# Attention and two feed-forward layers on one core: batch 0's loads in buffers of their own, issued at the start on two queues

## Chip, cores and metric

The kernel runs on one core of one Trainium2 chip. The metric is device time in microseconds (us). Three runs of the kernel before gave a median of 914.42 us (913.56 to 915.66).

## What is computed

Three stages follow each other: an attention with two kinds of causal window, and two feed-forward layers that feed each other. Cut to what matters:

```python
# q, k, v: (4, 8, 576, 64); heads 0-3: window of 32; heads 4-7: every 4th key of the last 128
scores = scale * q @ k.T
scores = where(mask, scores, -1e9)
attn = exp(scores - max(scores)); attn /= sum(attn) + 1e-9
x = (attn @ v), heads joined                   # (2304, 512)
h = x @ w_in;  g = max(h, 0) + alpha * min(h, 0);  x = g @ w_out      # d_ff 2048
h = x @ w2_in; g = 0 for h <= -1, h for h >= 1, (h + 1)**2 / 4 between;  y = g @ w2_out
```

The weights arrive as float64 words and are made into float32 on the chip.

## The kernel before

**Attention.** A batch has six groups (`NGB`); a group is 3 super-blocks of 128 query rows with 64 keys each. Per group: `a_scores` (TensorE: 4 mask matmuls, 12 score matmuls; VectorE: the row maximum), `a_exp` (L133), `a_turn` (three transposes on TensorE, a copy on ScalarE), `a_values` (12 matmuls, then three VectorE operations), `a_out` (three transposes, copies into `X` on ScalarE). A group needs two operand tiles. `qk` holds queries and keys; its lower 64 partitions and its upper 64 partitions are loaded by one DMA each (`a_load_qk`, L96), the rest of the tile is zeroed by memsets at the start (L352, L353). `vz` holds the values and is loaded likewise (`a_load_v`, L102; memsets L354, L355). In batch 0 three buffers of each serve six groups, so a later group's load waits for the reads of an earlier one. All of these DMAs are issued by SyncE's queue, in program order.

**Weights.** A piece is a 128x512 block of float64 words, 512 KB. `w_load` (L193) brings it into `st` (two buffers), `w_make` (L199) gives three VectorE operations (L224, L225, L219), and `conv(k)` (L372) runs the next `k` of them; when a piece is done the next one's load is issued. A layer has 32 pieces, 96 operations. An input piece is then cut into a high and a low part (`w_cut`, L229, POOL making the low part), an output piece in `wo_split`.

**Feed-forward.** A layer has five token tiles; a tile has 16 slots (`NF`), one per 128 columns of d_ff. A slot runs `f_h` (12 matmuls), `f_g` (VectorE, and `gh` on ScalarE, L293), `f_cut`, and two slots later `f_y` (12 matmuls).

**Order.** The program is laid out by hand (`manual_schedule`): each engine runs its instructions in the order of the code. The start is the loop over the six groups of batch 0 (from L389), then the first matmuls of slots 0 and 1, with `conv` calls between. In the first tile, `conv` runs 1 operation in slot 0 (`EARLY[0]`), 6 in slot 1 and 6 in each later slot until the 32 pieces are made. Attention of the other batches is spread over the slots.

**Waits of DMAs.** Transfers issued on the hardware queues share eight completion semaphores, in turn. A DMA that takes a semaphore waits, on the engine that issues it, until the DMA that had the semaphore before has landed. These waits stand in the built program, not in the source.

Of the kernel before, what the change touches and what calls it, by code (L numbers as in the profile page):

```python
# [10 lines left out]
F32 = mybir.dt.float32  # L11
# [21 lines left out]
KW = 192  # L33
# [3 lines left out]
KQ = GS * KW  # L37
QK = KQ + GS * P
# [9 lines left out]
# operations that make weights: in the first two slots; inside f_g and before f_cut, by phase  # L48
EARLY = (1, 6)
BEFORE = ((0, 3), (1, 3))  # L50
# points from the scores of a group to its transposes, its values and its output
# [3 lines left out]
def _subs(sb):  # L55
    """The four (head pair, sub-block) of a super-block of a batch."""
    base = 0 if sb < NSB // 2 else 2
    n = 4 * (sb % (NSB // 2))
    return [(base + (n + j) // NSUB, (n + j) % NSUB) for j in range(4)]


def _key_offset(sb, j):
    return 32 * j + (32 if sb % (NSB // 2) == NSB // 4 and j >= 2 else 0)
# [3 lines left out]
def attention_then_two_ffns(ctx: ExitStack, tc: tile.TileContext, aqk, av, w1i, w1o, w2i, w2o, alpha, masks, ident, out):  # L67
# [22 lines left out]
    sc_t, s_t, pT_t, o_t = {}, {}, {}, {}  # L90

    def buf(i):
        """The first batch has three buffers for its operands, the others two."""
        return i % 3 if i < NGB else i % 2

    def a_load_qk(i):  # L96
        if i < NG:
            t = qk[buf(i)]
            nc.sync.dma_start(t[:D, :QK], aqk[i, :D])
            nc.sync.dma_start(t[D:, KQ:], aqk[i, D:])  # L100

    def a_load_v(i):  # L102
        if i < NG:
            for h in range(2):
                r = slice(h * D, (h + 1) * D)
                nc.sync.dma_start(vz[buf(i)][r, :, h].rearrange("p n j d -> p n (j d)"), av[i, r])

    def a_scores(i, pool, tag, add_on_pe):
        ps = pool.tile([P, GS, 2, KEYS], F32, tag=tag, name="s_ps")
        sb0 = (i % NGB) * GS  # L110
        t = qk[buf(i)]
        mk = mask[:, sb0:sb0 + GS, None, :].to_broadcast([P, GS, 2, KEYS])
        if add_on_pe:
            for j in range(4):
                r = slice(j * SUB, (j + 1) * SUB)
                nc.tensor.matmul(ps[r], idb[:, r], mk, start=True, stop=False)
        for n in range(GS):
            for j in range(4):
                k0 = _key_offset(sb0 + n, j)
                r = slice(j * SUB, (j + 1) * SUB)  # L120
                q = t[:, KQ + n * P + j * SUB:KQ + n * P + (j + 1) * SUB]
                k = bass.AP(t.tensor, t.offset + n * KW + k0, [t.ap[0], [QK, 2], [1, KEYS]])
                nc.tensor.matmul(ps[r, n], q, k, start=not add_on_pe, stop=not add_on_pe or n == GS - 1)
        s = tmp(i).tile([P, 2 * GS, KEYS], F32, tag="s", name="s")
        src = ps.rearrange("p n h k -> p (n h) k")
        if not add_on_pe:
            nc.vector.tensor_tensor(s.rearrange("p (n h) k -> p n h k", h=2), ps, mk, ALU.add)
            src = s
        mx = st_p.tile([P, 2 * GS], F32, tag="mx", name="mx")
        nc.vector.tensor_reduce(mx, src, AX.X, ALU.max)  # L130
        sc_t[i] = (src, s, mx)

    def a_exp(i):  # L133
        src, s, mx = sc_t.pop(i)
        nc.vector.tensor_scalar(mx, mx, -SCALE, None, ALU.mult)
        for n in range(2 * GS):
            nc.scalar.activation(s[:, n], src[:, n], AF.Exp, bias=mx[:, n:n + 1], scale=SCALE)
        s_t[i] = s
# [52 lines left out]
    wt, wo, cv, cut = {}, {}, {}, []  # L191

    def w_load(ph, f, part):  # L193
        w = ((w1i, w1o), (w2i, w2o))[ph][part]
        st = cv_p.tile([P, DM, 2], I32, tag="st", name="st")
        nc.sync.dma_start(st.rearrange("p a b -> p (a b)"), w[f].bitcast(I32))
        cv[ph, f, part] = st

    def w_make(ph, f, part):  # L199
        """The three operations that make a piece: sign and highest exponent bit, the 27 bits behind the  # L200
        three exponent bits that float32 lacks, the top of the low word (0 and float32's normal range)."""
        st = cv.pop((ph, f, part))
        top, low = st[:, :, 1], st[:, :, 0]
        if part:
            wf = wp.tile([P, DM], F32, tag=f"o{f}", name="wo")
            wo[ph, f] = wf
        else:
            hi = wp.tile([P, DM], F32R, tag=f"ih{f}", name="wih")
            lo = wp.tile([P, DM], F32R, tag=f"il{f}", name="wil")
            if (ph, f) == (0, 1):  # L210
                # the second piece is made before the first is cut
                wf = wp.tile([P, DM], F32, tag=f"o{NF - 1}", name="wf")
            else:
                wf = cv_p.tile([P, DM], F32, tag="wf", name="wf", bufs=1)
            wt[ph, f] = (hi, lo)
        wi = wf.bitcast(I32)

        def last():
            nc.vector.scalar_tensor_tensor(wi, low, 29, wi, ALU.logical_shift_right, ALU.bitwise_or)  # L219
            if not part:  # L220
                cut.append((wf, hi, lo))

        return [
            lambda: nc.vector.tensor_scalar(wi, top, 0x07FFFFFF, 3, ALU.bitwise_and, ALU.logical_shift_left),  # L224
            lambda: nc.vector.scalar_tensor_tensor(wi, top, -0x40000000, wi, ALU.bitwise_and, ALU.bitwise_or),  # L225
            last,
        ]
# [98 lines left out]
    def pieces(ph):  # L326
        """The order in which the weights are needed."""
# [5 lines left out]
    with tc.manual_schedule(), ExitStack() as late:  # L333
        first = ExitStack()
        sp = first.enter_context(tc.tile_pool(name="sp", bufs=1))
        qk.append(sp.tile([P, QK + KQ], F32, tag="qk2", name="qk2"))
        vz.append(sp.tile([P, GS, 2, 4, DS], F32, tag="vz2", name="vz2"))
# [11 lines left out]
        nc.scalar.activation(half, half, AF.Exp, scale=0.0)  # L349
        nc.scalar.activation(half, half, AF.Copy, scale=0.5)  # L350
        for i in range(3):
            nc.vector.memset(qk[i][:D, QK:], 0.0)  # L352
            nc.vector.memset(qk[i][D:, :KQ], 0.0)  # L353
            nc.gpsimd.memset(vz[i][:D, :, 1], 0.0)  # L354
            nc.gpsimd.memset(vz[i][D:, :, 0], 0.0)  # L355
        a_load_qk(0)
        a_load_qk(1)
        a_load_v(0)
        a_load_qk(2)
        a_load_v(1)  # L360
        a_load_v(2)
# [3 lines left out]
        # the tensor engine reaches its full clock while the first loads are under way  # L365
# [6 lines left out]
        def conv(k):  # L372
            """The next k operations that make weights; behind each piece another load starts."""
# [13 lines left out]
        # the attention of batch 0 alone; the first products run while its last heads are still under way  # L387
        n0 = order[0]
        for i in range(NGB):  # L389
            a_scores(i, ps_h, "h", True)  # L390
            a_load_qk(i + 3 if i < 5 else i + 2)
            if i < 2:
                w_load(*pend_l.pop(0))
            if i >= 3:
                a_out(i - 3, ps_y, f"y{2 + i % 2}")
            if i >= 1:
                a_turn(i - 1, ps_a, "a")
            a_exp(i)
            if i == 5:
                conv(1)  # L400
                w_cut(True)
                x_split(n0, 0, True)
                conv(1)
            if i >= 2:
                a_values(i - 2, ps_y, f"y{i % 2}")
                a_load_v(i + 1)
            if i == 3:
                conv(2)
        conv(1)
        a_values(4, ps_y, "y0")  # L410
        a_load_v(7)
        a_turn(5, ps_a, "a")
        a_out(3, ps_y, "y3")
        conv(1)
        x_split(n0, 1, True)
        w_cut(True)
        a_values(5, ps_y, "y1")
        a_out(4, ps_y, "y2")
        x_split(n0, 2)
        f_h(n0, 0, (0,))  # L420
        a_out(5, ps_y, "y3")
        x_split(n0, 3)
        f_h(n0, 0, (1,))
        f_h(n0, 1, (0, 1))
# [36 lines left out]
        for k in range(len(slots) + 2):  # L461
            n, f = slots[k] if k < len(slots) else (None, None)
            nn = order[k // NF + 1] if k // NF + 1 < len(order) else None
            # the results of a tile leave before the next but one needs its banks
# [11 lines left out]
            if n:  # L476
# [5 lines left out]
                elif n == n0:  # L482
                    ops = 6
# [46 lines left out]
def _attention_layout(q, k, v):  # L530
    """Super-blocks of four sub-blocks of 32 queries of a head pair; heads 4-7 by residue of the position."""
# [9 lines left out]
    ak = np.zeros((B, NSB, P, KW), q.dtype)  # L541
    av = np.ones((B, NSB, P, 4, DS), q.dtype)
    for sb in range(NSB):
        for j, (hp, s) in enumerate(_subs(sb)):
            p0 = s * SUB
            aq[:, sb, :, j * SUB:(j + 1) * SUB] = q[:, hp, :, p0:p0 + SUB].transpose(0, 1, 3, 2).reshape(B, P, SUB)
            k0 = _key_offset(sb, j)
            ak[:, sb, :, k0:k0 + KEYS] = k[:, hp, :, p0:p0 + KEYS].transpose(0, 1, 3, 2).reshape(B, P, KEYS)
# [5 lines left out]
    aq, ak, av = groups(aq), groups(ak), groups(av)  # L554
# [38 lines left out]
```

## Time and profile before

| | us |
|---|---|
| median of the runs | 914.42 |
| lowest and highest run | 913.56, 915.66 |
| span of the profiled execution | 912.2 |
| TensorE busy in it | 872.4 |
| VectorE busy | 543.0 |
| ScalarE busy | 338.3 |
| GpSimd busy | 264.3 |

The page gives the profiled execution by its span alone; the span is 2.2 us below the median of the runs, which also hold what lies around it. The engine shares are averages over the start (attention of batch 0), the first tile (weights are made), and the long rest.

### The profile page before, as it was taken

To read this page: it belongs to the slowest core of one execution; us is meant where nothing else is said; L and a number is where in the kernel's file an instruction comes from. 1 tells how busy PE (TensorE), PEld (TensorE's weight loads), DVE (VectorE), ACT (ScalarE), POOL (GpSimd) and SP (SyncE) were. 2 spreads that over 40 slices of the span, in tenths; PEclk is the share of its full clock that TensorE was granted. 3 is DMA by queue.
4 is the path that set the end of the run, shared out by engine and by line. 5 is a ranking of instruction groups with operands and counts; after the bars stand their busy time and mean duration, and the time that the engine had idled before them with its cause. 6 is when DMAs were issued, how large, how long until landed. Compare 5 with 4: busy or idle time off the path is not lost.

```text
span 912.2 us, 13342 instructions
## 1 busy us (share of the span) xinstructions
PE 872.4 (96%) x5194; PEld 716.2 (79%) x5194; DVE 543.0 (60%) x872; ACT 338.3 (37%) x693; POOL 264.3 (29%) x208
## 2 busy tenths in 40 slices
PE   6789888999999999999999999999999999999998
PEld 3567666788888888998777777888888888888898
DVE  3599999744455444447999897443354335433443
ACT  3533334433343332333222433343343334333454
POOL 3223333121221212443434343222212222222243
PEclk7999999999999999999999999999999999999999
DMA  9956654312213200000333131010001000100000
GB/s 224 229 178 198 188 178 155 78 41 50 70 40 79 65 1 1 1 1 27 135 126 129 69 139 70 1 47 0 1 1 47 0 1 1 47 1 0 29 19 24
DMA packets 26319, 61.38 MB, mean 67 GB/s; under 512 B 2976, under 2 KB 12736, under 8 KB 26256
## 3 DMA queue, kind: packets, MB, share of 16 engines
q1 hardware_dynamic: 26080, 60.16, 22.6%
q8 instruction: 41, 0.67, 0.3%
q0 software_dynamic: 176, 0.37, 0.2%
q14 instruction: 22, 0.18, 0.1%
HBM read 55.80 MB, written 4.72 MB: 66 GB/s over the span
## 4 chain that ended last, share of the span: by engine, by line
PE 72%; DVE 18%; DMA 5%; issue 3%; ACT 1%; SPq 1%; POOL 0%; ACTq 0%; DVEq 0%
PE h_ps L274 12%; PE y L311 11%; PE h_ps L276 11%; PE h_ps L275 11%; PE y L312 11%; PE y L313 11%; DVE wo L225 4%; DVE gl L299 2%; DMA st<-w1i 2%; DVE wo L219 2%; DMA vz<-av 2%; DVE wf L224 2%; DVE wf L225 2%; DVE g L286 2%; DVE wo L224 1%
## 5 line engine op out<-in xcount | busy, mean ns | idle before, releaser
L261 POOL TENSOR_TENSOR wol<-wo,woh 128x512 fp32r<-128x512 f32 x160 | 213.1, 1332 | 512.7 <-ACT woh L260 512.6
L274 PE MATMUL h_ps<-xh,wil 128*128 128x512 f32 (+1 forms) x640 | 242.2, 378 | 15.0 <-DVE gl L299 7.7
L311 PE MATMUL y<-gh,wol 128*128 128x512 f32 (+1 forms) x640 | 238.7, 373 | 5.0 <-POOL wol L261 5.0
L276 PE MATMUL h_ps<-xh,wih 128*128 128x512 f32 (+1 forms) x640 | 237.8, 372 | 0.0
L275 PE MATMUL h_ps<-xl,wih 128*128 128x512 f32 (+1 forms) x640 | 236.4, 369 | 1.3 <-DVE xl L248 1.3
L312 PE MATMUL y<-gh,woh 128*128 128x512 f32 (+1 forms) x640 | 236.1, 369 | 0.0
L313 PE MATMUL y<-gl,woh 128*128 128x512 f32 (+1 forms) x640 | 235.7, 368 | 0.0
L293 ACT ACTIVATE gh<-h_ps 128x512 fp32r<-128x512 f32 (+1 forms) x160 | 88.8, 555 | 245.8 <-PE y L312 147.8
L299 DVE TENSOR_TENSOR gl<-h_ps,gh 128x512 fp32r<-128x512 f32 (+1 forms) x160 | 101.8, 636 | 119.2 <-ACT gh L293 118.3
L274 PEld LDWEIGHTS h_ps<-xh,wil 128*128 128x128 f32 x640 | 120.7, 189 | 44.1 <-DVE gl L299 10.2
L311 PEld LDWEIGHTS y<-gh,wol 128*128 128x128 f32 x640 | 120.4, 188 | 30.6 <-POOL wol L261 9.3
L275 PEld LDWEIGHTS h_ps<-xl,wih 128*128 128x128 f32 x640 | 120.9, 189 | 22.5 <-DVE xl L248 2.1
L276 PEld LDWEIGHTS h_ps<-xh,wih 128*128 128x128 f32 x640 | 120.7, 189 | 22.3
L313 PEld LDWEIGHTS y<-gl,woh 128*128 128x128 f32 x640 | 120.3, 188 | 20.8
L312 PEld LDWEIGHTS y<-gh,woh 128*128 128x128 f32 x640 | 120.4, 188 | 19.5
L260 ACT ACTIVATE woh<-wo 128x512 fp32r<-128x512 f32 x160 | 99.7, 624 | 33.0 <-DVE wo L219 33.0
L290 ACT ACTIVATE g<-g,half 128x512 f32<-128x512 f32 (+1 forms) x80 | 54.5, 681 | 146.8 <-DVE g L289 146.6
L289 DVE TENSOR_SCALAR g<-h_ps 128x512 f32<-128x512 f32 (+1 forms) x80 | 50.7, 634 | 67.1 <-PE h_ps L276 66.9
L292 DVE TENSOR_TENSOR h_ps<-h_ps,g 128x512 f32<-128x512 f32 (+1 forms) x80 | 51.7, 646 | 60.2 <-ACT g L290 60.2
L286 DVE TENSOR_SCALAR g<-h_ps,al 128x512 f32<-128x512 f32 (+1 forms) x80 | 55.4, 692 | 41.0 <-PE h_ps L276 41.0
L236 POOL TENSOR_TENSOR wil<-wf,wih 128x512 fp32r<-128x512 f32 x32 | 41.9, 1311 | 125.6 <-ACT wih L235 97.7
L287 DVE SCALAR_TENSOR_TENSOR h_ps<-h_ps,g 128x512 f32<-128x512 f32 (+1 forms) x80 | 51.7, 646 | 2.7
(53 smaller groups left out, 509.2 us busy)
## 6 DMA issues: line engine op xcount, KB each, us to landing
qk<-aqk SPq DMA_DIRECT2D x50, 240.0 KB, 4.8
vz<-av SPq DMA_DIRECT2D x48, 195.0 KB, 5.3
st<-w1i SPq DMA_DIRECT2D x16, 512.0 KB, 3.4
st<-w1o SPq DMA_DIRECT2D x16, 512.0 KB, 3.2
st<-w2i SPq DMA_DIRECT2D x16, 512.0 KB, 3.2
st<-w2o SPq DMA_DIRECT2D x16, 512.0 KB, 3.2
out_t<-X SPq DMA_DIRECT2D x16, 256.0 KB, 2.0
out_t<-X SPq DMA_DIRECT2D x4, 128.0 KB, 1.8
```

Source lines behind the costliest of these rows:

```text
L225: lambda: nc.vector.scalar_tensor_tensor(wi, top, -0x40000000, wi, ALU.bitwise_and, ALU.bitwise_or),
L260: nc.scalar.activation(hi, wf, AF.Copy)
L261: nc.gpsimd.tensor_tensor(lo, wf, hi.bitcast(F32), ALU.subtract)
L274: nc.tensor.matmul(ps[:, :w], wl[:, cs], xh[:, :w], start=(c == 0), stop=False)
L275: nc.tensor.matmul(ps[:, :w], wh[:, cs], xl[:, :w], start=False, stop=False)
L276: nc.tensor.matmul(ps[:, :w], wh[:, cs], xh[:, :w], start=False, stop=(c == NC - 1))
L286: nc.vector.tensor_scalar(t, ps, 0.0, al[:, f:f + 1], ALU.min, ALU.mult)
L293: nc.scalar.activation(hi, ps, AF.Copy)
L299: nc.vector.tensor_tensor(lo, ps, hi.bitcast(F32), ALU.subtract)
L311: nc.tensor.matmul(o, wl[:, cs], gh, start=(f == 0), stop=False)
L312: nc.tensor.matmul(o, wh[:, cs], gh, start=False, stop=False)
L313: nc.tensor.matmul(o, wh[:, cs], gl, start=False, stop=(f == NF - 1))
```

## The change

Each of batch 0's six groups gets a `qk` and a `vz` buffer of its own (`buf`), and all their loads stand at the head of the program, the lower 64 partitions on SyncE's queue and the upper 64 on ScalarE's (`second`). Five weight pieces are loaded among them, in halves in the same way; three of them (`EST`) get `st` buffers of their own. These DMAs stand ahead of ScalarE's first activation. Keys that super-blocks of a group share are loaded once (`KW`: a `qk` half goes from 960 to 832 columns). The zeroing of buffers 2 to 5 goes to POOL. In batch 0's loop, `a_exp` takes `at_once`: VectorE subtracts the row maximum in one operation and ScalarE makes one exponential of 384 columns in place of six of 64. The loop's order is new, `conv(3)` stands in each turn from the second on, and the cut of input pieces goes from VectorE to ScalarE there. `EARLY` is (5, 6), and later slots of the first tile run 5 or 6 operations in turn. Weight buffers from slot 8 on (`NE`) move to a pool opened after batch 0's buffers are closed.

```diff
-KW = 192
-KQ = GS * KW
-QK = KQ + GS * P
+KW = 4 * GS * SUB + 2 * WIN
+QW = GS * P
+QK = KW + QW
+NE = 8
+EST = (2, 3, 4)
-EARLY = (1, 6)
+EARLY = (5, 6)
...
     def buf(i):
-        return i % 3 if i < NGB else i % 2
+        return i if i < NGB else i % 2
+
+    def second(i):
+        return nc.scalar if i < NGB else nc.sync
...
             nc.sync.dma_start(t[:D, :QK], aqk[i, :D])
-            nc.sync.dma_start(t[D:, KQ:], aqk[i, D:])
+            second(i).dma_start(t[D:, KW:], aqk[i, D:])
...
-                nc.sync.dma_start(vz[buf(i)][r, :, h].rearrange("p n j d -> p n (j d)"), av[i, r])
+                q = second(i) if h else nc.sync
+                q.dma_start(vz[buf(i)][r, :, h].rearrange("p n j d -> p n (j d)"), av[i, r])
...
+        if at_once:
+            nc.vector.tensor_tensor(s, src, mx[:, :, None].to_broadcast([P, 2 * GS, KEYS]), ALU.subtract)
+            nc.scalar.activation(s, s, AF.Exp, scale=SCALE)
+            s_t[i] = s
+            return
...
-        st = cv_p.tile([P, DM, 2], I32, tag="st", name="st")
-        nc.sync.dma_start(st.rearrange("p a b -> p (a b)"), w[f].bitcast(I32))
+        own = ph == 0 and pieces(0).index((ph, f, part)) in EST
+        st = (sp if own else cv_p).tile([P, DM, 2], I32, tag="sx" if own else "st", name="st", bufs=len(EST) if own else 2)
+        src = w[f].bitcast(I32)
+        if len(pend_l) > 2 * NF - 6 and ph == 0:
+
+            nc.sync.dma_start(st[:D].rearrange("p a b -> p (a b)"), src[:D])
+            nc.scalar.dma_start(st[D:].rearrange("p a b -> p (a b)"), src[D:])
+        else:
+            nc.sync.dma_start(st.rearrange("p a b -> p (a b)"), src)
...
-        qk.append(sp.tile([P, QK + KQ], F32, tag="qk2", name="qk2"))
-        vz.append(sp.tile([P, GS, 2, 4, DS], F32, tag="vz2", name="vz2"))
+        for i in range(2, NGB):
+            qk.append(sp.tile([P, QK + KW], F32, name=f"qk{i}"))
+            vz.append(sp.tile([P, GS, 2, 4, DS], F32, name=f"vz{i}"))
...
+        pend_l = pieces(0)
+        pend_w = list(pend_l)
+
+        a_load_qk(0)
+        a_load_v(0)
+        for i in range(1, NGB):
+            a_load_qk(i)
+            w_load(*pend_l.pop(0))
+            a_load_v(i)
         nc.scalar.activation(half, half, AF.Exp, scale=0.0)
         nc.scalar.activation(half, half, AF.Copy, scale=0.5)
-        for i in range(3):
-            nc.vector.memset(qk[i][:D, QK:], 0.0)
-            nc.vector.memset(qk[i][D:, :KQ], 0.0)
+        for i in range(NGB):
+            z = nc.vector if i < 2 else nc.gpsimd
+            z.memset(qk[i][:D, QK:], 0.0)
+            z.memset(qk[i][D:, :KW], 0.0)
             nc.gpsimd.memset(vz[i][:D, :, 1], 0.0)
             nc.gpsimd.memset(vz[i][D:, :, 0], 0.0)
-        a_load_qk(0)
-        a_load_qk(1)
-        a_load_v(0)
-        a_load_qk(2)
-        a_load_v(1)
-        a_load_v(2)
...
         for i in range(NGB):
...
+            if i >= 1:
+                a_turn(i - 1, ps_a, "a")
+            a_scores(i, *((ps_h, "h") if i < 4 else (ps_a, "a")), True)
+            if i < 2:
+                a_load_qk(i + NGB)
+            w_cut()
+            a_exp(i, True)
+            if i >= 1:
+                a_values(i - 1, ps_y, f"y{i % 2}")
+                if i < 3:
+                    a_load_v(i - 1 + NGB)
             if i >= 2:
+                a_out(i - 2, ps_y, f"y{2 + i % 2}")
+            if i >= 1:
+                conv(3)
+            if i >= 4:
+                x_split(n0, i - 4, True)
+        f_h(n0, 0, (0,))
+        a_turn(NGB - 1, ps_a, "a")
+        a_out(NGB - 2, ps_y, "y2")
+        f_h(n0, 0, (1,))
+        w_cut()
+        a_values(NGB - 1, ps_y, "y0")
         x_split(n0, 2)
...
         first.close()
+        wl_p = late.enter_context(tc.tile_pool(name="wl_p", bufs=1))
...
                 elif n == n0:
-                    ops = 6
+                    ops = 5 + f % 2
```

The order that results, at the two places that matter. First ScalarE, from the start of the program; before, its first work is the activations (names: `half` is a constant, `s` the scores of a group, `pT` the turned scores):

```order
L349 ACT_TABLE_LOAD
L349 ACTIVATE half_89<-half_89 128x1 [waits DVE_49]
L350 ACTIVATE half_89<-half_89 128x1 [waits Activation_49]
L137 ACTIVATE s_162<-s_ps_145,mx_163 128x64 [waits DVE_49,PE_49]
L137 ACTIVATE s_162<-s_ps_145,mx_163 128x64 x5
L146 ACTIVATE pT_204<-t_ps_200 128x384 [waits PE_49]
```

In the change 17 DMA issues stand there first; these are the last eight of them and what follows (`DMAHW` is one of the eight completion semaphores):

```order
L219 DMA st_134<-w1i 64x1024 [waits DMAHW2_49]
L116 DMA vz3_102<-av 64x3x260 [waits DMAHW4_49]
L109 DMA qk4_103<-aqk 64x832 [waits DMAHW6_49]
L219 DMA st_141<-w1o 64x1024 [waits DMAHW0_49]
L116 DMA vz4_104<-av 64x3x260 [waits DMAHW2_49]
L109 DMA qk5_105<-aqk 64x832 [waits DMAHW4_49]
L219 DMA st_148<-w1i 64x1024 [waits DMAHW6_49]
L116 DMA vz5_106<-av 64x3x260 [waits DMAHW0_49]
L384 ACT_TABLE_LOAD
L384 ACTIVATE half_89<-half_89 128x1 [waits DVE_49]
L385 ACTIVATE half_89<-half_89 128x1 [waits Activation_49]
L147 ACTIVATE s_207<-s_207 128x384 [waits DVE_49]
```

On ScalarE's queue a semaphore comes back after four DMAs, so each issue from the fifth on waits for the landing of the fourth before it; the last one (`vz5`) waits for `st_141`, the half of a weight piece that stands four ahead. The table load and group 0's exponential moved behind that.

Second VectorE, one turn of batch 0's loop. Before, the fifth group:

```order
L130 TENSOR_REDUCE mx_351<-s_ps_333 128x6
L135 TENSOR_SCALAR mx_351<-mx_351 128x6
L158 TENSOR_SCALAR rs_388<-o_ps_374 128x6
L159 RECIPROCAL rs_388<-rs_388 128x6
L160 TENSOR_TENSOR o_387<-o_ps_374,rs_388 128x384
```

In the change, the same group:

```order
L140 TENSOR_REDUCE mx_421<-s_ps_403 128x6
L146 TENSOR_TENSOR s_420<-s_ps_403,mx_421 128x384
L173 TENSOR_SCALAR rs_441<-o_ps_427 128x6
L174 RECIPROCAL rs_441<-rs_441 128x6
L175 TENSOR_TENSOR o_440<-o_ps_427,rs_441 128x384
L249 TENSOR_SCALAR wo_450<-st_141 128x512
L250 SCALAR_TENSOR_TENSOR wo_450<-st_141,wo_450 128x512
L244 SCALAR_TENSOR_TENSOR wo_450<-st_141,wo_450 128x512
```

A wide subtraction has taken the place of the small `L135`, and a whole weight piece stands in the turn.

## Rows read from the trace of the kernel before

**Rows 1.** Windows: stretch, each engine's busy us (x instructions), granted clock, DMA share, GB/s

```profile
0.00:5.00 5.00, 3.80 (x10) 1.26 (x10) 3.24 (x8) 1.69 (x3) 3.90 (x10) 1.00 0.60 143
...
100.00:150.00 50.00, 44.93 (x322) 34.15 (x314) 48.56 (x74) 17.52 (x43) 15.92 (x13) 1.00 0.61 186
...
200.00:300.00 100.00, 100.00 (x704) 81.37 (x703) 49.97 (x90) 36.58 (x89) 20.85 (x16) 1.00 0.23 55
```

**Rows 2.** Waits, 0 to 60 us, SyncE's queue: us in total, times, longest

```profile
SPq L99 <- DMA st<-w1i: 3.1, 1, 3.1
```

**Rows 3.** Timeline of SyncE's queue: start us, us, engine, line, tile

```profile
0.75 0.57 SPq L99 DMA_DIRECT2D qk<-aqk  x1
...
5.86 4.09 SPq L106 DMA_DIRECT2D vz<-av  x4
```

**Rows 4.** DMAs: packets, MB of GpSimd's queue; KB of each issue, us to landing

```profile
q0 software_dynamic: 176, 0.37, 0.2%
...
qk<-aqk SPq DMA_DIRECT2D x50, 240.0 KB, 4.8
vz<-av SPq DMA_DIRECT2D x48, 195.0 KB, 5.3
...
st<-w1i SPq DMA_DIRECT2D x16, 512.0 KB, 3.4
```

**Rows 5.** Windows of 2 us, columns as in rows 1

```profile
12.00:14.00 2.00, 0.76 (x16) 0.79 (x20) 0.00 (x0) 0.62 (x4) 0.00 (x0) 0.50 1.11 226
...
18.00:20.00 2.00, 1.29 (x24) 1.08 (x24) 0.09 (x1) 0.00 (x0) 0.00 (x0) 0.50 1.09 332
...
44.00:46.00 2.00, 2.00 (x11) 1.51 (x9) 0.17 (x1) 1.52 (x7) 1.29 (x1) 1.00 1.00 350
```

**Rows 6.** Timeline, ScalarE's start and the exponentials of groups 0 and 5

```profile
0.75 1.28 ACT L349 ACT_TABLE_LOAD   x1 [0.75 <-PEq L573]
...
2.28 0.20 ACT L350 ACTIVATE half<-half 128x1 f32<-128x1 f32 x1
...
8.37 1.34 ACT L137 ACTIVATE s<-s_ps,mx 128x64 f32<-128x64 f32 x6 [5.89 <-DVE mx L135]
...
30.84 1.33 ACT L137 ACTIVATE s<-s_ps,mx 128x64 f32<-128x64 f32 x6
```

**Rows 7.** Groups by form, 0 to 60 us: busy us, mean ns, idle before

```profile
L130 DVE TENSOR_REDUCE mx<-s_ps 128x6 f32<-128x384 f32 x8 | 4.4, 555 | 12.5 <-PE s_ps L123 12.5
...
L160 DVE TENSOR_TENSOR o<-o_ps,rs 128x384 f32<-128x384 f32 x7 | 3.9, 558 | 0.2
L146 ACT ACTIVATE pT<-t_ps 128x384 f32<-128x384 f32 x7 | 3.5, 504 | 7.4 <-PE t_ps L144 7.4
...
L219 DVE SCALAR_TENSOR_TENSOR wf<-st,wf 128x512 int32<-128x512 int32 x4 | 2.7, 687 | 0.1
...
L354 POOL MEMSET vz<- 64x780 f32 x3 | 2.3, 750 | 0.1
...
L224 DVE TENSOR_SCALAR wf<-st 128x512 int32<-128x512 int32 x4 | 1.7, 420 | 0.0
```

**Rows 8.** Timeline, TensorE's scores of a group at either clock

```profile
13.24 1.51 PE L123 MATMUL s_ps<-qk 128*32 128x128 f32 x24 [2.10 <-DMA qk<-aqk]
...
28.41 0.86 PE L123 MATMUL s_ps<-qk 128*32 128x128 f32 x24 [1.78 <-DMA qk<-aqk]
```

**Rows 9.** Timeline, from the last groups to the first slot's `gh`

```profile
33.95 0.87 PE L155 MATMUL o_ps<-vz,pT 128*32 128x130 f32 x24 [2.90 <-DMA vz<-av]
...
41.04 0.69 DVE L248 TENSOR_TENSOR xl<-X,xh 128x512 fp32r<-128x512 f32 x1 [0.42 <-ACT xh L247]
...
46.74 0.45 DVE L224 TENSOR_SCALAR wo<-st 128x512 int32<-128x512 int32 x1 [2.55 <-DMA st<-w1o]
...
49.51 0.60 ACT L293 ACTIVATE gh<-h_ps 128x512 fp32r<-128x512 f32 x1 [2.89 <-DMA st<-w1i]
```

**Rows 10.** Timeline, first tile, a weight operation beside GpSimd's work

```profile
102.99 1.66 DVE L225 SCALAR_TENSOR_TENSOR wo<-st,wo 128x512 int32<-128x512 int32 x1
```

More of the change, by code (lines that the diff above doesn't have):

```diff
@@ L59, in _subs, with _key_offset @@
     return [(base + (n + j) // NSUB, (n + j) % NSUB) for j in range(4)]
-def _key_offset(sb, j):
-    return 32 * j + (32 if sb % (NSB // 2) == NSB // 4 and j >= 2 else 0)
+def _key_offset(g, m):
+    return SUB * m + (WIN if g % 3 == 1 and m >= 6 else 0)
 @with_exitstack
@@ L85, in attention_then_two_ffns @@
     idb = idt.bitcast(BF16).rearrange("p (k two) -> p k two", two=2)[:, :, 1]
-    qk = [const.tile([P, QK + KQ], F32, name=f"qk{i}") for i in range(2)]
+    qk = [const.tile([P, QK + KW], F32, name=f"qk{i}") for i in range(2)]
     vz = [const.tile([P, GS, 2, 4, DS], F32, name=f"vz{i}") for i in range(2)]
@@ L118, in a_scores @@
             for j in range(4):
-                k0 = _key_offset(sb0 + n, j)
+                k0 = _key_offset(i % NGB, 4 * n + j)
                 r = slice(j * SUB, (j + 1) * SUB)
-                q = t[:, KQ + n * P + j * SUB:KQ + n * P + (j + 1) * SUB]
-                k = bass.AP(t.tensor, t.offset + n * KW + k0, [t.ap[0], [QK, 2], [1, KEYS]])
+                q = t[:, KW + n * P + j * SUB:KW + n * P + (j + 1) * SUB]
+                k = bass.AP(t.tensor, t.offset + k0, [t.ap[0], [QK, 2], [1, KEYS]])
                 nc.tensor.matmul(ps[r, n], q, k, start=not add_on_pe, stop=not add_on_pe or n == GS - 1)
@@ L131, in a_scores, with a_exp @@
         sc_t[i] = (src, s, mx)
-    def a_exp(i):
+    def a_exp(i, at_once=False):
         src, s, mx = sc_t.pop(i)
+        if at_once:
[3 more added lines that the diff above has]
+            return
         nc.vector.tensor_scalar(mx, mx, -SCALE, None, ALU.mult)
@@ L191, in attention_then_two_ffns, with w_pool @@
     wt, wo, cv, cut = {}, {}, {}, []
+    def w_pool(f):
+        return wp if f < NE else wl_p
     def w_load(ph, f, part):
         w = ((w1i, w1o), (w2i, w2o))[ph][part]
-        st = cv_p.tile([P, DM, 2], I32, tag="st", name="st")
-        nc.sync.dma_start(st.rearrange("p a b -> p (a b)"), w[f].bitcast(I32))
+        own = ph == 0 and pieces(0).index((ph, f, part)) in EST
[6 more added lines that the diff above has]
+            nc.sync.dma_start(st.rearrange("p a b -> p (a b)"), src)
         cv[ph, f, part] = st
@@ L204, in w_make @@
         if part:
-            wf = wp.tile([P, DM], F32, tag=f"o{f}", name="wo")
+            wf = w_pool(f).tile([P, DM], F32, tag=f"o{f}", name="wo")
             wo[ph, f] = wf
         else:
[L208 to L212, printed above, removed]
+            hi = w_pool(f).tile([P, DM], F32R, tag=f"ih{f}", name="wih")
+            lo = w_pool(f).tile([P, DM], F32R, tag=f"il{f}", name="wil")
+            if ph == 0 and f in (1, 3):
+                wf = sp.tile([P, DM], F32, tag="wx", name="wf")
             else:
@@ L348, in attention_then_two_ffns @@
         nc.vector.memset(half, 0.5)
+        pend_l = pieces(0)
[6 more added lines that the diff above has]
+            a_load_v(i)
         nc.scalar.activation(half, half, AF.Exp, scale=0.0)
         nc.scalar.activation(half, half, AF.Copy, scale=0.5)
-        for i in range(3):
-            nc.vector.memset(qk[i][:D, QK:], 0.0)
-            nc.vector.memset(qk[i][D:, :KQ], 0.0)
+        for i in range(NGB):
+            z = nc.vector if i < 2 else nc.gpsimd
+            z.memset(qk[i][:D, QK:], 0.0)
+            z.memset(qk[i][D:, :KW], 0.0)
             nc.gpsimd.memset(vz[i][:D, :, 1], 0.0)
             nc.gpsimd.memset(vz[i][D:, :, 0], 0.0)
-        a_load_qk(0)
-        a_load_qk(1)
-        a_load_v(0)
-        a_load_qk(2)
-        a_load_v(1)
-        a_load_v(2)
-        pend_l = pieces(0)
-        pend_w = list(pend_l)
         ps = ps_y.tile([P, TW], F32, tag="y0", name="warm_ps")
@@ L389, in attention_then_two_ffns @@
         for i in range(NGB):
[L390 to L395, printed above, removed]
             if i >= 1:
                 a_turn(i - 1, ps_a, "a")
[L398 to L403, printed above, removed]
-            if i >= 2:
[L405 to L418, printed above, removed]
+            a_scores(i, *((ps_h, "h") if i < 4 else (ps_a, "a")), True)
[7 more added lines that the diff above has]
+                    a_load_v(i - 1 + NGB)
+            if i >= 2:
+                a_out(i - 2, ps_y, f"y{2 + i % 2}")
[9 more added lines that the diff above has]
+        a_values(NGB - 1, ps_y, "y0")
         x_split(n0, 2)
-        f_h(n0, 0, (0,))
-        a_out(5, ps_y, "y3")
+        f_h(n0, 1, (0, 1))
+        a_out(NGB - 1, ps_y, "y3")
         x_split(n0, 3)
-        f_h(n0, 0, (1,))
-        f_h(n0, 1, (0, 1))
         conv(3)
@@ L540, in _attention_layout @@
     aq = np.zeros((B, NSB, P, P), q.dtype)
-    ak = np.zeros((B, NSB, P, KW), q.dtype)
+    ak = np.zeros((B, NGB, P, KW), q.dtype)
     av = np.ones((B, NSB, P, 4, DS), q.dtype)
@@ L546, in _attention_layout @@
             aq[:, sb, :, j * SUB:(j + 1) * SUB] = q[:, hp, :, p0:p0 + SUB].transpose(0, 1, 3, 2).reshape(B, P, SUB)
-            k0 = _key_offset(sb, j)
-            ak[:, sb, :, k0:k0 + KEYS] = k[:, hp, :, p0:p0 + KEYS].transpose(0, 1, 3, 2).reshape(B, P, KEYS)
+            g, n = divmod(sb, GS)
+            k0 = _key_offset(g, 4 * n + j)
+            ak[:, g, :, k0:k0 + KEYS] = k[:, hp, :, p0:p0 + KEYS].transpose(0, 1, 3, 2).reshape(B, P, KEYS)
             av[:, sb, :, j, :D] = v[:, hp, :, p0:p0 + KEYS].reshape(B, P, D)
@@ L552, in groups @@
         return a.reshape(NG, GS, P, -1).transpose(0, 2, 1, 3).reshape(NG, P, -1)
-    aq, ak, av = groups(aq), groups(ak), groups(av)
+    aq, ak, av = groups(aq), ak.reshape(NG, P, KW), groups(av)
     lower = np.concatenate([ak[:, :D], aq[:, :D]], axis=2)
```

## Prediction

> **What bounds the kernel now.** I read the windows first. From 200 us TensorE is busy all the time, so a change of the start is worth what it moves the point at which that stretch begins. Between 100 and 150 us VectorE is busy 48.56 of 50 us and TensorE 44.93: the first tile, where weights are made, is set by VectorE more than by TensorE [rows 1]. The reader is to see that work moved off VectorE there is worth something, and that TensorE can win back at most the rest.
>
> Then the start. SyncE's queue waits for landings: a DMA with nothing to do with weights waited 3.1 us until a weight piece had landed [rows 2], and four issues that take 0.57 each took 4.09 together [rows 3]. An issue that has to wait holds its engine. Of the start I note four times [rows 6, 9]: group 0's exponentials begin at 8.37, group 5's end at 30.84 + 1.33 = 32.17, the first tile is split (last `xl`) at 41.73, and slot 0's `gh` begins at 49.51.
>
> **The change, step by step.**
>
> 1. *ScalarE's issues.* Before the table load ScalarE now issues 17 DMAs, and the last waits for the landing of its half of the fourth weight piece. What has been moved by then on both queues: 5 `qk` groups of 2 x 208 KB (240 KB x 832/960 [rows 4]), 4 `vz` groups of 2 x 195 and 4 pieces of 512, 5688 KB or 5.82 MB, and 0.37 MB of constants: 6.19 MB. In the first 5 us 0.72 MB move (143 GB/s) [rows 1]. The rate of the rest is the unknown. From below: 226 GB/s, a window in which half tiles alone are on the way, one after the other; from above: 350, with weight pieces, and 332 in another such window [rows 5]. Those pieces write all 128 partitions at once; two queues that each write one half resemble them more than half tiles in a row, but value tiles are among them, which the upper windows hardly have, so I take 300. Then 5 + 5.47/0.3 = 23.2 us; one issue (0.57 [rows 3]) and the stretch of table load and small activations (0.75 to 2.48, 1.73 [rows 6]) put group 0's exponential at **25.5** instead of 8.37, 17.1 later. At 226 GB/s it would be 31.5, at 350 22.9. The issues themselves (17 x 0.57 = 9.7) hide inside that wait; if the wait were gone they would decide (below).
>
> The Trainium skill, "DMA: Bandwidth & Descriptors", section "Rules for kernel authors", speaks against the two queues: transfers to disjoint halves of the partitions share the same engines either way and "serialize". By it the rate would stay with the half tiles in a row; that is the second rival.
>
> 2. *The groups after it.* Their operands have landed by then, so the pace is that of the engines. VectorE per group: maximum 0.56, subtraction 0.56 (not in the trace as such; nearest the 128x384 operation of L160), the three operations of the values 0.16 + 0.19 + 0.56 (the two small ones by the timeline around that row), weights 0.42 + 2 x 0.69 [rows 7]: 3.8, with hand-overs 4.1. The chain exponential, turn, scores, maximum, subtraction is about as long at full clock; at the half clock (0.50 where TensorE has little to do [rows 5]) scores take 1.51 instead of 0.86 [rows 8] and a turn about 1 us more. TensorE stands still from about 8 to 26 us, so I let two turns run at the half clock: 0.5 + 4.8 + 5.1 + 3 x 4.1 = 22.7, group 5's exponential ends at 48.2, **16.0 later** than 32.17. The exponential in one piece (bounded by the 0.50 of the 128x384 copy [rows 7] against 1.33) only shortens ScalarE's part, which isn't what is waited for.
>
> 3. *To the split of the first tile.* Before 9.56 us, 2.90 of them a wait for values [rows 9] that are long there now. But three weight operations (1.8) now stand ahead of the last values on VectorE: 9.56 - 2.90 + 1.8 = 8.5. The split is done at 56.7, 15.0 later.
>
> 4. *To slot 0's `gh`.* Before 7.78, with 2.55 of VectorE waiting for a weight piece [rows 9]; that piece is now requested during the loop. 5.2 are left: `gh` at 61.9, **12.4 later**.
>
> 5. *The first tile.* At that point 20 of 96 weight operations are done instead of 11. Nine fewer are 9 x 0.6 = 5.4 us of VectorE, and up to 1 us more per piece, as an operation beside GpSimd takes 1.66 instead of 0.69 [rows 10]: 8 us at most, nothing at least. The slots get 5 or 6 operations instead of 6, but slot 0 gets 5 instead of 1, and what VectorE saves TensorE has to make up in its 5 idle us per 50 [rows 1]. I take 3. **Net +9.4.**
>
> Costed at nothing: GpSimd's memsets (12 of 0.75 [rows 7], 8 of about 0.45: done by 17 us, before the first turn; without that cover the third group's scores would wait for them, a few us); the memsets and casts that VectorE loses (2.4 us) against what its wider subtractions add (6 x 0.4); the smaller loads of later batches, whose DMA queues are idle; the new pool of weights, first used when the buffers under it are long read. Next late after step 4 is VectorE again.
>
> **Sum.** 17.1 - 1.1 - 1.0 - 2.6 - 3.0 = +9.4 on the profiled execution: 912.2 + 9.4 = 921.6, which is 2.2 below the runs: **924**. A measurement of this kernel tells about 0.2% (1.8 us) from no change.
>
> **Rivals.**
>
> *First tile absorbs it.* VectorE's full 8 us come back: 924 - 5 = 919; with the rate at 350 as well, 916. For it: 48.56 of 50. Against: TensorE has only 5 us in 50 to give, and a fixed number of operations stands in each slot. Chance 0.18.
>
> *Two queues bring nothing* (the rule cited above). The trace has no two hardware queues at once, so no run here shows it; the nearest row for it is the 226 of half tiles. Group 0's exponential at 31.5, 6 later: 930. Chance 0.20.
>
> *ScalarE is not held* (the other side). If the waits cost ScalarE nothing, because landings keep ahead of its issues, its 17 issues end at 0.75 + 9.7, group 0's exponential stands at 12.2, and the groups are paced by landings: the last `qk` at 5 + (7.02 - 0.72)/0.3 = 26.0, group 5's exponential ends at about 28.5, 3.7 earlier than now; with steps 3 to 5 (-1.1, -2.6, -3.0) 10 less: 904. The forecast turns to this side when group 0's exponential comes before 25.5 - 9.4 = 16 us. For that 5.47 MB would have to move in 9 us, 600 GB/s, where 350 is the most the rows show; so only a wait that doesn't hold the engine would do it, and SyncE's rows speak against that. Chance 0.07.
>
> That the change does not do what it says is part of my forecast: only four DMAs per queue are issued early, the rest when landings let them.
>
> **How the numbers follow.** Forecast (ScalarE held, rate near 300) 0.52; the rivals 0.18, 0.20, 0.07; 0.03 for more than these (a half clock that lasts). The time is the forecast's, 924. Its own bounds: rate -2.6 and +6, clock -2 and +2, first tile -5 and +3, together about 917 to 933. The range, 915 to 935, takes in both rivals that are slower and leaves out the fast one and the tails. Faster by over 0.2%: 0.07 and a little of the first rival, 0.10; within 0.2%: 0.07; slower: 0.83.
>
> **What would show it.** Right: the timeline has ScalarE without work until 22 to 31 us, the waits of its DMAs on landings in the list of waits, TensorE's first turn right behind it, the granted clock at 0.5 around 20 us; group 5 done near 48, slot 0's `gh` near 62; windows from 5 to 25 us near 300 GB/s. Wrong: an exponential before 16 us, or `gh` of slot 0 before 50; a rate near 226 gives the second rival; a first tile that takes 8 us less than before gives the first.

## The result and the profile after

The change takes **927.59 us** (median of 4 runs, 926.21 to 931.02), beside 914.74 for the kernel before on the same chip: ratio 1.0146, 95% interval 1.0130 to 1.0163. The profiled execution has a span of 924.4 us, 12.2 more than the 912.2 of before. The prediction was 924 (915 to 935), slower.

The windows of the change, 10 to 40 us, show the new hole (columns as in [rows 1]):

```profile
10.00:15.00 5.00, 0.00 (x0) 0.00 (x0) 0.27 (x1) 0.00 (x0) 4.67 (x9) 0.50 1.07 283
15.00:20.00 5.00, 0.00 (x0) 0.00 (x0) 0.00 (x0) 0.00 (x0) 1.92 (x3) 0.50 1.06 231
20.00:25.00 5.00, 0.00 (x0) 0.00 (x0) 0.00 (x0) 0.00 (x0) 0.00 (x0) 0.50 1.07 227
25.00:30.00 5.00, 0.00 (x0) 0.00 (x0) 0.00 (x0) 0.56 (x1) 0.00 (x0) 0.50 1.07 228
30.00:35.00 5.00, 3.37 (x51) 2.59 (x55) 0.63 (x2) 2.03 (x5) 0.00 (x0) 0.50 1.06 230
35.00:40.00 5.00, 4.46 (x68) 2.84 (x60) 4.21 (x9) 1.65 (x3) 0.77 (x1) 0.50 1.07 232
```

From 20 to 25 us no engine computes. Only the DMAs run, at a share of 1.07, and they move 227 GB/s. The granted clock is 0.50, the 1.2 GHz level, while TensorE stands still and up to 40 us. ScalarE's timeline says what holds the others:

```profile
2.91 0.62 ACTq L219 DMA_DIRECT2D st<-w1i  x1
5.27 0.56 ACTq L116 DMA_DIRECT2D vz<-av  x1
...
18.82 0.47 ACTq L109 DMA_DIRECT2D qk<-aqk  x1
...
28.84 0.56 ACTq L116 DMA_DIRECT2D vz<-av  x1
29.44 1.28 ACT L384 ACT_TABLE_LOAD   x1 [29.44 <-DMA st<-w1o]
...
31.07 0.51 ACT L147 ACTIVATE s<-s 128x384 f32<-128x384 f32 x1
...
52.59 0.52 ACT L147 ACTIVATE s<-s 128x384 f32<-128x384 f32 x1 [2.70 <-DVE s L146]
...
66.06 0.60 ACT L318 ACTIVATE gh<-h_ps 128x512 fp32r<-128x512 f32 x1 [0.20 <-DVE h_ps L312]
```

Four DMAs go out back to back. The fifth (5.27) to the seventeenth (28.84) each wait for a landing. The table load, at 0.75 before [rows 6], ends a wait of 29.44 us for a half of `st<-w1o`, the semaphore that the order had shown. The first exponential follows at 31.07 instead of 8.37, the last one ends at 53.11 instead of 32.17, and slot 0's `gh` begins at 66.06 instead of 49.51 [rows 6, 9]. The list of waits, 0 to 60 us, shows who stood behind ScalarE (engine, line, what released it; us in total, times, longest):

```profile
DVE mx L140 <- PE s_ps L133: 30.3, 3, 24.1
ACT L384 <- DMA st<-w1o: 29.4, 1, 29.4
...
PE t_ps L159 <- ACT s L147: 26.7, 5, 22.6
```

TensorE's first turn waits for ScalarE, group 1's scores stand behind that turn on TensorE, and VectorE's next maximum waits for those scores.

Did the early issues at least bring data sooner? The DMA view of the first 31 us, of before:

```profile
DMA packets 3672, 7.02 MB, mean 226 GB/s; under 512 B 476, under 2 KB 2395, under 8 KB 3670
```

and of the change:

```profile
DMA packets 3830, 6.99 MB, mean 225 GB/s; under 512 B 528, under 2 KB 2480, under 8 KB 3830
```

The same 7.0 MB. The DMA engines were at a full share in the kernel before too (1.02 to 1.10 in the windows from 5 to 30 us): over the 31 us, issuing early and on a second queue moved no byte more. It changed which bytes come first (weight pieces now lie among the groups' operands) and who waits. The rate was not even over that time, though. The change again, in windows that part at 14 us:

```profile
9.00:14.00 5.00, 0.04 (x4) 0.00 (x0) 1.11 (x2) 0.00 (x0) 4.67 (x9) 0.58 1.06 294
14.00:30.00 16.00, 0.00 (x0) 0.00 (x0) 0.00 (x0) 0.56 (x1) 2.84 (x5) 0.50 1.07 229
```

The DMA view shows the two queues (q1 is SyncE's, with the lower halves, q10 ScalarE's, with the upper ones; packets, MB, share of the engines). From 12 to 13 us both are at work, and they move 348 GB/s:

```profile
DMA packets 205, 0.35 MB, mean 348 GB/s; under 512 B 33, under 2 KB 131, under 8 KB 205
q1 hardware_dynamic: 102, 0.21, 67.3%
q10 hardware_dynamic: 103, 0.13, 45.7%
```

Later they mostly take turns. From 16.0 to 16.5 us nearly all packets are SyncE's, from 21.0 to 21.5 all are ScalarE's:

```profile
q1 hardware_dynamic: 98, 0.10, 105.5%
q10 hardware_dynamic: 5, 0.00, 1.3%
...
DMA packets 31, 0.13 MB, mean 254 GB/s; under 512 B 0, under 2 KB 0, under 8 KB 31
q10 hardware_dynamic: 31, 0.13, 106.5%
```

After the start, between 100 and 150 us, VectorE's share is smaller and TensorE's larger:

```profile
100.00:150.00 50.00, 47.19 (x345) 37.97 (x345) 45.94 (x74) 19.27 (x49) 20.22 (x15) 1.00 0.63 187
```

TensorE is busy 2.26 us more than before (44.93 [rows 1]), though by then each kernel is at another place of its program.

### The profile page after: what moved, and what is told of

Its sections match the earlier page's. It is cut to its first block, busy times and chain, and to the rows that moved or that the text cites. A ratio compares the mean times of both kernels' runs of the same rounds, so it can differ in the third digit from the quotient of the medians.

```text
span 924.4 us, 13303 instructions
## 1 busy us (share of the span) xinstructions
PE 871.6 (94%) x5194; PEld 714.8 (77%) x5194; DVE 536.7 (58%) x868; ACT 332.8 (36%) x665; POOL 275.5 (30%) x222
## 4 chain that ended last, share of the span: by engine, by line
PE 71%; DVE 16%; DMA 7%; issue 3%; ACT 2%; POOL 0%; SPq 0%; ACTq 0%; DVEq 0%
PE h_ps L299 12%; PE y L336 11%; PE h_ps L301 11%; PE h_ps L300 11%; PE y L338 11%; PE y L337 11%; DMA st<-w1o 3%; DVE wo L250 3%; DVE gl L324 2%; DVE wo L244 2%; DVE g L311 1%; PE s_ps L133 1%; DMA qk<-aqk 1%; DVE wf L250 1%; DVE h_ps L312 1%
## 5 line engine op out<-in xcount | busy, mean ns | idle before, releaser
L286 POOL TENSOR_TENSOR wol<-wo,woh 128x512 fp32r<-128x512 f32 x160 | 215.6, 1349 | 513.8 <-ACT woh L285 508.5
L301 PEld LDWEIGHTS h_ps<-xh,wih 128*128 128x128 f32 x640 | 120.3, 188 | 22.4
```

What stands on the lines that cost most here:

```text
L286: nc.gpsimd.tensor_tensor(lo, wf, hi.bitcast(F32), ALU.subtract)
L301: nc.tensor.matmul(ps[:, :w], wh[:, cs], xh[:, :w], start=False, stop=(c == NC - 1))
```

## The experiments

Two questions were open. Is ScalarE's wait the whole loss, or does the new content of the loop cost something too? And what sets the rate of about 230 GB/s: the number of queues, or the transfers themselves? The theory was that ScalarE is held by its own DMAs' semaphores and that a second queue adds no rate. The rivals stand with each expectation. All ratios are to the kernel before on the same chip (914.33 us for the first four runs, 914.39 for the last four).

**All loads on SyncE.** The change with nothing but the queue undone.

```diff
     def second(i):
-        return nc.scalar if i < NGB else nc.sync
+        return nc.sync
...
-            nc.scalar.dma_start(st[D:].rearrange("p a b -> p (a b)"), src[D:])
+            nc.sync.dma_start(st[D:].rearrange("p a b -> p (a b)"), src[D:])
```

> All of batch 0's loads on SyncE's queue, the rest of the change kept. Theory (ScalarE is held by the waits of its DMAs): group 0's exponential stands near 10 us instead of 31.07, the groups are paced by landings at about 230 GB/s, group 5's exponential near 34 instead of 52.6, slot 0's gh near 52 instead of 66; 907 to 914 us, 14 to 20 less than the change. Rival (the new loop, with a weight piece and a wide subtraction in each turn, costs the time): the time stays at 922 or more. On the rate: if two queues bring nothing, the windows from 5 to 30 us show the same 230 GB/s here; if they help, it is lower here.

Measured: 915.04 us (912.27 to 917.16), ratio 1.0007 [0.9996, 1.0018], span 912.5. Its windows, and ScalarE's first and last exponential of batch 0 with slot 0's `gh`:

```profile
10.00:15.00 5.00, 3.52 (x55) 2.36 (x55) 3.05 (x7) 1.18 (x3) 4.70 (x8) 0.65 1.09 241
15.00:20.00 5.00, 3.60 (x52) 3.08 (x53) 2.90 (x7) 1.15 (x2) 3.33 (x5) 0.50 1.06 234
20.00:25.00 5.00, 2.75 (x40) 2.05 (x42) 2.01 (x5) 1.84 (x3) 1.28 (x1) 0.50 1.06 231
```

```profile
8.51 0.52 ACT L147 ACTIVATE s<-s 128x384 f32<-128x384 f32 x1 [6.04 <-DVE s L146]
...
37.17 0.52 ACT L147 ACTIVATE s<-s 128x384 f32<-128x384 f32 x1 [3.80 <-DVE s L146]
...
51.58 0.60 ACT L318 ACTIVATE gh<-h_ps 128x512 fp32r<-128x512 f32 x1 [0.79 <-DVE h_ps L312]
```

Issuing the 17 upper halves from ScalarE costs the whole 1.4%. From 15 to 25 us one queue moves 234 and 231 GB/s here where two moved 231 and 227: there the second queue adds no rate. From 10 to 15 us two moved 283, and one moves 241. The Trainium skill, "DMA: Bandwidth & Descriptors", section "Rules for kernel authors", says of two transfers to disjoint halves of the partitions that they serialize, from one engine or from two; the trace of the change agrees from 14 us on (229 GB/s) and not from 9 to 14 (294). The groups now wait for landings (group 5 ends at 37.69, 5.5 later than before, as weight pieces are ahead of its operands), and what the later steps give back makes that good: no change against before. The time lies 1 us above the range expected and 12.6 below the change, where 14 to 20 were expected; group 5's exponential came 3 us later than expected.

**The first four, eight or twelve upper halves on ScalarE, the rest on SyncE.** The first four take semaphores that nobody holds; from the fifth on each waits.

```diff
+    on_act = [4]
+
+    def upper():
+        on_act[0] -= 1
+        return nc.scalar if on_act[0] >= 0 else nc.sync
+
     def second(i):
-        return nc.scalar if i < NGB else nc.sync
+        return upper() if i < NGB else nc.sync
...
-            nc.scalar.dma_start(st[D:].rearrange("p a b -> p (a b)"), src[D:])
+            upper().dma_start(st[D:].rearrange("p a b -> p (a b)"), src[D:])
```

Four:

> Only the first four upper halves on ScalarE's queue (none of them waits for a landing), the other 13 on SyncE's. Theory: ScalarE is free at 3.5 us, so within 2 us of the kernel with all loads on SyncE's queue (907 to 914). Rival (any DMA on ScalarE's queue costs): 920 or more.

Eight (`on_act = [8]`):

> The first eight upper halves on ScalarE, the rest on SyncE; weight pieces in halves. Theory (ScalarE is held until the DMA four places ahead of its last one has landed): ScalarE's table load at 12 to 13.5 us, group 0's exponential at 14 to 15.5, slot 0's gh at 51 to 53, 912 to 915 us, between the runs with four (912.92) and twelve (917.37). Rival (the price is per issue on ScalarE, not the wait: a third of the way from 4 to 17 issues): the exponential at 8.5 + 8 x 1.3 = 19, gh near 55 and 917.

Twelve (`on_act = [12]`):

> The first 12 upper halves on ScalarE's queue, the last 5 on SyncE's: a shorter hold. In the change ScalarE's 12th issue stands at 18.8 us, so ScalarE is free at 19.3 and group 0's exponential stands at 21 instead of 31.07. Theory: 7 to 10 us less than the change, 917 to 921. Rival (the loop's content costs the time): 925 or more.

| upper halves on ScalarE | table load | first exponential | slot 0's `gh` | median us | ratio to before |
|---|---|---|---|---|---|
| 0 | 0.75 | 8.51 | 51.58 | 915.04 | 1.0007 [0.9996, 1.0018] |
| 4 | 3.29 | 10.80 | 51.52 | 912.92 | 0.9986 [0.9976, 0.9996] |
| 8 | 12.83 | 14.47 | 51.57 | 912.13 | 0.9976 [0.9965, 0.9986] |
| 12 | 19.33 | 20.97 | 55.41 | 917.37 | 1.0033 [1.0022, 1.0044] |
| 17 (the change) | 29.44 | 31.07 | 66.06 | 927.59 | 1.0146 [1.0130, 1.0163] |

ScalarE's timeline with eight:

```profile
12.24 0.56 ACTq L122 DMA_DIRECT2D vz<-av  x1
12.83 1.28 ACT L390 ACT_TABLE_LOAD   x1 [12.83 <-DMA st<-w1i]
...
14.47 0.51 ACT L153 ACTIVATE s<-s 128x384 f32<-128x384 f32 x1
```

and with twelve:

```profile
18.83 0.47 ACTq L115 DMA_DIRECT2D qk<-aqk  x1
19.33 1.28 ACT L390 ACT_TABLE_LOAD   x1 [19.33 <-DMA vz<-av]
...
20.97 0.51 ACT L153 ACTIVATE s<-s 128x384 f32<-128x384 f32 x1
```

With eight and with twelve the table load starts as the last issue ends, and what that issue had waited for is the DMA four places ahead. The eighth issue in the change's own trace, at 12.19, stands where it stands here. A fixed price per issue, the rival of the run with eight, would have put the first exponential at 19; it came at 14.47. Up to eight the hold is free: the last groups wait for their operands anyway, group 5's exponential begins at 37.17, 37.36 and 36.95 with none, four and eight, and `gh` stays at 51.5. From eight on the hold shows in `gh`: 3.8 us later for a first exponential 6.5 later from eight to twelve, then 10.65 for 10.1, one for one. The time with eight (912.13) was expected between those with four and twelve; it is level with four, as the two intervals overlap.

**Weight pieces whole, all on SyncE.** The change's five early pieces in one DMA of 128 partitions each, in place of two of 64.

```diff
-        if len(pend_l) > 2 * NF - 6 and ph == 0:
+        if False:
```

(and `second` as in the first run)

> All loads on SyncE's queue, and the five weight pieces by one DMA of 128 partitions each. Theory on the rate (a DMA of 64 partitions goes at 230 GB/s, one of 128 at 330): 2.6 MB take 8 us instead of 11.4, the last values land 3 to 3.5 us earlier than with halves, 904 to 911 us, 2 to 4 less than with halves. Rival (230 GB/s is the rate of everything at the start): no difference to the kernel with halves, within 1 us.

Measured: 911.07, ratio 0.9966 [0.9950, 0.9981]; a second time 911.67, 0.9968 [0.9956, 0.9980]. Windows of the first:

```profile
10.00:15.00 5.00, 3.94 (x55) 2.99 (x55) 2.61 (x7) 0.72 (x2) 4.70 (x8) 0.50 1.06 276
15.00:20.00 5.00, 3.01 (x62) 2.01 (x58) 4.64 (x10) 2.65 (x5) 3.36 (x5) 1.00 1.07 274
20.00:25.00 5.00, 2.83 (x58) 2.01 (x58) 3.69 (x9) 2.34 (x5) 1.31 (x1) 1.00 1.07 257
```

With the queue the same and the bytes the same, 128-partition pieces raise 231 to 241 GB/s to 257 to 276 from 10 to 25 us, and slot 0's `gh` comes at 49.08 instead of 51.58. The time is 4 us less than with halves, as expected, and this is faster than both kernels. The second time stood for this expectation:

> The version with all early loads on SyncE and whole weight pieces once more, beside the one with three upper halves on ScalarE on the same chip: 909 to 913 us, ratio to the kernel before 0.995 to 0.998.

**Operands whole as well.** Each `qk` and `vz` tile of batch 0 too is loaded by one DMA to 128 partitions. Same bytes in half as many DMAs; the upper partitions' queries, keys and values land in other columns, so the run leaves out batch 0's right scores and values. The memsets zero the columns that are not loaded, at the same sizes.

```diff
             t = qk[buf(i)]
+            if i < NGB:
+                nc.sync.dma_start(t[:, :QK], aqk[i])
+                return
...
         if i < NG:
+            if i < NGB:
+                nc.sync.dma_start(vz[buf(i)][:, :, 0].rearrange("p n j d -> p n (j d)"), av[i])
+                return
...
-            z.memset(qk[i][D:, :KW], 0.0)
+            z.memset(qk[i][D:, QK:], 0.0)
...
-            nc.gpsimd.memset(vz[i][D:, :, 0], 0.0)
+            nc.gpsimd.memset(vz[i][D:, :, 1], 0.0)
```

(and `second` and the weight pieces as in the run before)

> As the run with all early loads on SyncE and whole weight pieces (911.07 us, ratio 0.9966), but each qk and each vz tile of batch 0 is loaded by one DMA to all 128 partitions in place of two to 64. The bytes are the same. The queries, keys and values of the upper partitions land in columns where they aren't read as such, so batch 0's scores and values aren't the reference's; every instruction that reads them has the same shape. Theory: a DMA to 64 partitions is what holds the rate at about 230 GB/s, whichever queue issues it; then the windows from 5 to 25 us move 300 to 345 GB/s, the last values land near 22 to 24 us, group 5's exponential ends 3 to 6 us earlier than 34.5, and the time is 904 to 909. Rival: the rate is a matter of these transfers' own size (fewer than a weight piece's 512 KB) or of the queue; then the windows stay at 251 to 276 GB/s and the time at 910 to 912.

Measured: 909.37, ratio 0.9932 [0.9916, 0.9948]. Its windows:

```profile
5.00:10.00 5.00, 1.70 (x29) 1.18 (x28) 0.00 (x0) 0.00 (x0) 4.65 (x9) 0.80 0.99 343
10.00:15.00 5.00, 3.16 (x51) 2.18 (x47) 1.28 (x3) 1.01 (x2) 4.67 (x8) 0.50 1.04 400
15.00:20.00 5.00, 4.43 (x78) 2.94 (x70) 4.57 (x10) 1.65 (x3) 2.23 (x4) 0.67 1.05 386
20.00:25.00 5.00, 3.00 (x61) 2.29 (x61) 4.69 (x13) 3.30 (x7) 2.26 (x2) 1.00 1.06 330
```

On one queue, with transfers of 390 to 512 KB, the rate is 330 to 400 GB/s. In the same run, on the same queue, batch 1's operands then come in halves again, nearly alone from 26 to 28 us:

```profile
26.00:28.00 2.00, 1.25 (x31) 0.81 (x23) 1.86 (x5) 0.78 (x2) 0.57 (x1) 1.00 1.05 227
```

So one queue is enough for the high rate, and whole tiles in place of halves bring it. This run changes three things about a transfer at once: it writes 128 partitions, it is twice as large, and with eight semaphores twice as many bytes can be on the way. The 348 GB/s from 12 to 13 us in the change speak against the last two, as there all transfers were halves of 195 and 208 KB. They also show that halves are not bound to 230. Two queues at work at once are not enough for more, however: from 27 to 28 us of the change both moved packets, at 202 GB/s. What holds the halves at about 230 most of the time was not isolated.

The rate is more than I expected, the gain less: group 5's exponential starts at 32.62, only 1.9 before the 34.54 of the run with whole weight pieces, `gh` at 48.82 hardly moves, and the time lies 0.4 us above the range expected. Two waits in the trace take part of the rest. The identity matrix comes on GpSimd's queue beside the faster loads (6.5 us from issue to landing, 3.7 with weight pieces alone whole), and TensorE waits for it ahead of the first group:

```profile
8.51 0.51 PE L132 MATMUL s_ps<-mask,idt 128*32 128x384 bf16 x4 [3.30 <-DMA idt<-ident]
...
11.56 0.52 ACT L153 ACTIVATE s<-s 128x384 f32<-128x384 f32 x1 [9.08 <-DVE s L152]
...
24.05 0.52 ACT L153 ACTIVATE s<-s 128x384 f32<-128x384 f32 x1 [0.50 <-DVE s L152]
27.85 0.52 ACT L153 ACTIVATE s<-s 128x384 f32<-128x384 f32 x1 [0.50 <-DVE s L152]
```

And then VectorE paces the groups, 3.80 us apart in these two rows (3.8 to 4.8 over all six groups) and busy 4.69 of 5 us in the window from 20 us. The 2 us between this run's median and that of the whole weight pieces don't show in the profiled executions (`gh` 48.82 and 48.84, spans 909.1 and 908.1 beside each other); where they come from stays open.

**The best of both.** Whole weight pieces on SyncE, and the three upper halves that wait for no semaphore and aren't weights on ScalarE (`on_act = [3]` with `if False:`).

> Whole weight pieces on SyncE, and only the first three upper halves (qk0, vz0, qk1), which wait for no semaphore, on ScalarE. Theory (an issue costs ScalarE its 0.57 us and no more while it has no wait, and SyncE's queue is relieved of three issues): group 0's exponential at 8 to 10 us, slot 0's gh at 48 to 50, 909 to 912 us. Rival (two queues share the start badly, or ScalarE's issues delay the first exponential): exponential after 10.5, 912 to 915.

Measured: 910.21, ratio 0.9955 [0.9944, 0.9967], first exponential at 10.32, `gh` at 48.65. The exponential missed its range by 0.3 us, the rest held. Its interval overlaps that of the same kernel with all loads on SyncE (0.9968 [0.9956, 0.9980]): both beat both kernels, and which is better is not told apart.

## Why the prediction was right, and which term was mis-sized

The mechanism held: ScalarE's DMA issues stand ahead of its activations, the thirteen that wait hold it, and the groups start late. The total came nearer than its terms: step 1 was 5.6 us too small, and steps 2 to 5 gave back 2.8 more than the 7.7 forecast; that these misses partly cancel is luck. By its steps, in us of the profiled executions:

| step | from, to | before | after | difference | predicted |
|---|---|---|---|---|---|
| 1 | start, group 0's exponential | 8.37 | 31.07 | +22.7 | +17.1 |
| 2 | group 0's exponential, end of group 5's | 23.80 | 22.04 | -1.8 | -1.1 |
| 3 | that end, last `xl` of the split done | 9.56 | 7.93 | -1.6 | -1.0 |
| 4 | that, slot 0's `gh` | 7.78 | 5.02 | -2.8 | -2.6 |
| 5 | `gh`, end | 862.69 | 858.34 | -4.35 | -3.0 |
| | sum | 912.2 | 924.4 | +12.2 | +9.4 |

**Step 1, the rate: the term that was wrong in size.** I took 300 GB/s, on the ground that two queues which each write one half resemble a transfer to all 128 partitions. That was so from 9 to 14 us (294 GB/s) and not after it: to 30 us the queues mostly took turns, at 229. By 31 us 6.99 MB had moved; less 2.16 us at 230 GB/s, 6.49 MB by the last issue at 28.84. The first 5 us moved 0.68 MB (136 GB/s), so the other 5.81 MB took 23.84 us: 244 GB/s. Against 5 + 18.2 = 23.2 us as predicted, the rate costs 4.2 us (5.47 MB at 244 is 22.4 instead of 18.2) and 0.34 MB more than I counted 1.4 us (SyncE's queue was further ahead: its last issue stands at 27.70). The lower bound that I had kept, 226 GB/s and 31.5 us, came within 0.5 us of the 31.07 measured. The second rival, two queues bring nothing, thus came true in the main: the first exponential stood where it said. Its 930 was not reached, as the terms behind gave back more.

**Step 2** held, two turns at the half clock included: the windows to 40 us have 0.50. The turns are 4.45, 4.53, 3.98, 3.80 and 4.76 us long (predicted 4.8, 5.1 and three of 4.1). The last is long because a weight operation ran beside GpSimd, as in [rows 10]; in VectorE's timeline of the change (GpSimd runs a 128x512 operation from 49.60 to 50.88):

```profile
45.98 0.69 DVE L244 SCALAR_TENSOR_TENSOR wf<-st,wf 128x512 int32<-128x512 int32 x1
...
49.79 1.64 DVE L244 SCALAR_TENSOR_TENSOR wo<-st,wo 128x512 int32<-128x512 int32 x1
```

**Steps 3 and 4** held within 0.6 us: the waits for values and for the weight piece are gone, and `gh` now waits 0.20 for VectorE instead of 2.89 for a DMA [rows 9].

**Step 5** had the right sign; that the weight operations made earlier are its cause was not tried by a run of its own. From slot 0's `gh` to 200 us, in the kernel before and in the change:

```profile
49.51:200.00 150.49, 135.86 (x929) 105.65 (x930) 130.78 (x203) 57.19 (x135) 44.34 (x34) 0.99 0.51 149
66.06:200.00 133.94, 122.70 (x875) 97.25 (x868) 112.69 (x183) 51.88 (x125) 44.96 (x32) 1.00 0.51 148
```

TensorE is idle 14.63 us before and 11.24 in the change, which is 3.4 of the 4.35 us; the other 1.0 is not accounted for. The 4.35 are more than I took and less than the first rival's 8. That some of it comes back however the start runs is seen in the experiments, beside the 862.7 of before: from `gh` to the end it is 860.9 with all loads on SyncE (912.5 - 51.58), 859.0 with twelve on ScalarE (914.4 - 55.41), 858.8 with whole weight pieces (907.9 - 49.08).

**The third rival, that ScalarE is not held,** fell: but the point from which it was to decide, a first exponential before 16 us, lies where the runs put it, between eight halves (14.47, faster than before) and twelve (20.97, slower).

## What to carry to other kernels

A DMA that waits for a semaphore holds the engine that issues it: put on an engine that computes only as many as find a free semaphore, or as many as land before its first work could start anyway. Before loads are issued earlier or spread over queues, read whether the DMA engines are already busy in that stretch; here they were (the same 7.0 MB in 31 us), and what helped was another shape of the transfers. Of an unknown rate take the row with the same shape, not the one that the sum of two shapes resembles.

## What the hardware showed that I had not expected

From 5 to 25 us transfers to 64 partitions move 228 to 241 GB/s on one queue, and on two 227 to 243 but for one stretch, 283 from 10 to 15 us; the same bytes in transfers to 128 partitions move 330 to 400. The DMA share reads 0.99 to 1.09 in all of these, so a full share doesn't say that the rate is the highest one, and the packets are no smaller (6.99 MB in 3830 packets in the change's first 31 us, 1.8 KB each; 9.57 MB in 4957 packets in the run with whole operands, 1.9 KB). The Trainium skill, "DMA: Bandwidth & Descriptors", section "Rules for kernel authors", recommends one transfer to 128 partitions and gives as the reason that both halves use the same DMA engines. The advice agrees with these runs, 230 GB/s against 330 to 400. That the engines are shared does not by itself account for two halves being slower than the whole; what does was not tried.
